# Opening of a fused attention, MoE and gMLP kernel: weight conversions kept in order on VectorE, the first mixing product on ScalarE, the receive weight later

## The chip, the core and the metric

The kernel runs on one core of one Trainium2 chip. The metric is device time in microseconds (us) of one execution. Three runs of the kernel before gave 469.3, 469.85 and 469.86, so 469.85 is the median. Engines are named as the profile names them: PE is TensorE's matmul and PEld its weight load, DVE is VectorE, ACT is ScalarE, POOL is GpSimd, and SP is the queue that issues the DMAs.

## The reference

Three layers are applied one after another, all in float32, for 4 batches of 1088 tokens.

```python
# attention: 4 heads of 32; S1, S2 are (8, 32)
a, b = S1 @ x, S2 @ x                       # for x = q and x = k
phi(x) = outer(a, b).reshape(64)
kv, z = phi(k).T @ v, phi(k).sum(tokens)
x = (phi(q) @ kv) / (phi(q) @ z + 1e-6)     # joined to 128 columns
# token-mixing MLP; x_prev is x shifted by one token
xk = mu_k * x + (1 - mu_k) * x_prev
xr = mu_r * x + (1 - mu_r) * x_prev
x = sigmoid(xr @ w_r) * (relu(xk @ w_k) ** 2 @ w_v)     # w_k 128x1024, w_v 1024x128
# gMLP
u, v = split(relu(x @ w_in))                # 512 columns each
v = layernorm(v) ; v = w_spatial @ v + b    # w_spatial 1088x1088
out = (u * v) @ w_out
```

The weights of the two MLPs reach the chip as 64-bit floats, and the chip turns each into two 32-bit parts.

## The kernel before

Tokens lie along the columns in chunks of 384, 384 and 320 for each batch, twelve chunks in all, numbered i = 0 to 11. A float32 product is made of three matmuls (`mm3`, line 112): each operand is split into a high part H (a copy in the reduced matmul type) and a low part L (`low`, line 118, the difference), and low times high, high times high and high times low are added in PSUM. Both parts must be there before a triple is complete.

Weights pass through `split64` (lines 120 to 139). For a half of w_k or w_v (128x512) VectorE runs five steps: L125 takes the exponent bits, L127 and L128 gather the low mantissa bits, L129 puts the sign in, L130 makes the power of two. ScalarE turns the exponent around after L125 (line 126), scales the low bits after L128 (line 132) and copies the high part after L129 (line 115). GpSimd multiplies the low part after L130 (line 133). Five conversions matter here: the first and the second half of w_k (tiles k0 for H, k1 for L), the first and the second half of w_v (xs1H, xs1L) and the receive weight w_r (128x128, tiles wrH, wrL; its low part is made on VectorE, line 135).

The attention of chunk i has four steps: `q_feat` makes the outer products from a matmul with the small features (L189, L200), `q_turn` transposes them (L241, ScalarE copies them to tile VR), `q_num` multiplies by the key sums and divides (L258, L262 to L264), `q_out` transposes the result back to xT (L276, ScalarE copies it to tile x). `k_feat` and `k_sum` (L200, L220) do the same for keys. The outer products of the second batch's keys are three GpSimd products of 128x768 each.

`prep(i)` mixes the chunk with its shift and splits it. For chunk 0 `q_out` has also made mu_k * x (L280, `x_mu`), and `prep(0)` needs one more VectorE step (L300) to have xk; its H (m11, ScalarE, L115) and L (m13, VectorE, L118) go to the up matmuls. `prep_r` and `receive` do the same with mu_r and w_r, and `gate` takes the sigmoid.

The middle part counts groups g: `up(g)` multiplies chunk g // 8 by 128 columns of w_k (f = g % 8; f = 0 to 3 need the first half of w_k, f = 4 to 7 the second) into one of three PSUM banks, ScalarE takes the relu (L340). For every other group GpSimd squares it (L343) and `sqsplit` splits it (ScalarE L372, VectorE L118); for the others ScalarE squares it alone (L360) and a sum of both parts of w_v is used (`total_wv`, GpSimd, line 689, tile wvT; L386). `down(g)` follows four groups later and multiplies by w_v. Other work is hung on groups with `plan(g, fn)`; R0 and R1 say at which g the sums wvT, the conversions of the second half of w_v and of w_r and the receive work stand.

The code is not the order on the engines: a scheduling layer orders each engine's instructions with estimates of its own when the kernel is built, and each engine then runs its list strictly in that order. `behind(anchors, fn)` tells that layer not to place what fn records ahead of the anchor instructions in the list of the anchor's engine; it adds no wait on the chip.

Of the kernel before, what the change touches and what calls it, by code (L numbers as in the profile page):

```python
# [11 lines left out]
AF = mybir.ActivationFunctionType  # L12
ALU = mybir.AluOpType
# [45 lines left out]
W1G = 69  # L59
W1N = 8  # L60
ORD0 = ((0, 0), (1, 0), (0, 1), (1, 1), (2, 0), (3, 0), (2, 1), (3, 1), (0, 2), (1, 2), (2, 2), (3, 2))
R0 = (1, 5)
R1 = 5
VW = NH * (HD + 1)


# [1 line left out]
def attn_moe_gmlp(ctx: ExitStack, tc: tile.TileContext, qT, kT, va, st, wk, wv, wr, win, wout,  # L68
                  wT, wtail, btail, mu, ident, msk, out):
    nc = tc.nc  # L70
    TE, VE, SE, GE = nc.tensor, nc.vector, nc.scalar, nc.gpsimd
# [6 lines left out]
    def sb(tag, shape, dt=F32):  # L78
        uid[0] += 1
        return pool.tile(shape, dt, tag=tag, bufs=1, name=f"{tag}_{uid[0]}")  # L80
# [7 lines left out]
    def rot(*tags):  # L88
        i = count.get(tags, 0)
        count[tags] = i + 1  # L90
        return tags[i % len(tags)]
# [12 lines left out]
    mus = sb("mus", [128, 3])  # L104
# [12 lines left out]
    def low(eng, L, src, H):  # L117
        return eng.tensor_tensor(out=L, in0=src, in1=H.bitcast(F32), op=ALU.subtract)  # L118

    def split64(raw, n, H, L, total=None):  # L120
        hi, lo = raw[:, :, 1], raw[:, :, 0]
        x = rot(*CVT)
        th, s = sb(f"w{x + 1}", [128, 2, n], I32), sb(f"w{x + 2}", [128, n], I32)
        t, h = th[:, 0], th[:, 1]
        VE.tensor_scalar(out=t, in0=hi, scalar1=0x7FFFFFFF, scalar2=9, op0=ALU.bitwise_and, op1=ALU.logical_shift_right)  # L125
        SE.activation(out=h, in_=t, func=AF.Relu, scale=4096.0, bias=ebias)
        VE.tensor_scalar(out=s, in0=hi, scalar1=0x1FF, scalar2=15, op0=ALU.bitwise_and, op1=ALU.logical_shift_left)  # L127
        VE.scalar_tensor_tensor(out=s, in0=lo, scalar=17, in1=s, op0=ALU.logical_shift_right, op1=ALU.bitwise_or)  # L128
        VE.scalar_tensor_tensor(out=h, in0=hi, scalar=-0x80000000, in1=h, op0=ALU.bitwise_and, op1=ALU.bitwise_or)  # L129
        VE.tensor_scalar(out=t, in0=h, scalar1=-0x800000, scalar2=None, op0=ALU.bitwise_and)  # L130
        if total is None and n in CONVP:
            SE.activation(out=s.bitcast(F32), in_=s, func=AF.Copy, scale=2.0 ** -35)
            GE.tensor_tensor(out=L, in0=s.bitcast(F32), in1=t.bitcast(F32), op=ALU.mult)  # L133
        else:
            VE.scalar_tensor_tensor(out=L, in0=s, scalar=2.0 ** -35, in1=t.bitcast(F32), op0=ALU.mult, op1=ALU.mult)
        if total is None:
            copy(H, h.bitcast(F32))
        else:
            VE.tensor_tensor(out=total, in0=h.bitcast(F32), in1=L, op=ALU.add)
# [107 lines left out]
    nd_pe, x_copy, x_mu_op = [None], [None], [None]  # L247
# [19 lines left out]
    def q_out(i):  # L267
        b, c = divmod(i, 3)
        o, n = CH[c]
        if c == 0:  # L270
            xTs[b] = sb(f"x{b}", [128, S + 1])
            GE.memset(xTs[b][:, 0:1], 0.0)
        xm = qst.pop(i)
        px = bank(5)
        for t in order3(c):
            x_turn[0] = TE.transpose(px[:, cut(c, t)], xm[:, t].rearrange("p h c -> p (h c)"), idn)  # L276
        x_copy[0] = copy(xTs[b][:, 1 + o:1 + o + n], px[:, :n])
        if i == 0:
            a = x_mu[0] = sb(m(1), [128, n])
            x_mu_op[0] = VE.tensor_scalar(out=a, in0=px[:, :n], scalar1=mus[:, 0:1], scalar2=None, op0=ALU.mult)  # L280


    GL = B * NCH * NF - GLB
    anchor, prep_L = [None, None, None], [None, None]
# [329 lines left out]
    def behind(anchors, fn, *a):  # L614
        with ExitStack() as es:
            for x in anchors:
                es.enter_context(tc.issue_after(x.ins))
            fn(*a)
# [11 lines left out]
    nd_last0 = list(nd_last)  # L630
# [9 lines left out]
    behind(nd_pe0, k_sum, 1, 0, range(3))  # L640
    behind(x_turn0, k_sum, 1, 0, range(3, NT))
    k_sum(1, 1)
    behind(x_mu_op, conv64)
    load64(*wseq[4])
    load_q(1)
    behind(prep_L, conv64)
    prep_0 = list(prep_L) + PG * nd_pe0
    todo = {}

    def plan(g, fn, *a):  # L650
        todo.setdefault(g, []).append(lambda: fn(*a))
# [7 lines left out]
    for j in range(1, NI):  # L659
        sp = 1 if j < 3 else 2  # L660
        for n, fn in enumerate((q_feat, q_turn, q_num, q_out)):
            plan(QS[j] + sp * n, gated(fn) if j < 3 and n == 0 else fn, j)
        e = QS[j] + 3 * sp
        plan(max(8 * j - 6, e + 1), prep, j)
        plan(max(8 * j - 4, e + 2), prep_r, j)
        plan(8 * j - 2, receive, j)
        plan(8 * j - 1, gate, j)
    QE = [QS[3 * b + 2] + 1 for b in range(B)]
    for b in range(1, B):
        last = QS[3 * b]  # L670
# [23 lines left out]
    for n in range(2):  # L694
        plan(R0[n], total_wv, n)
        plan(R0[n], conv_first)
    plan(R1, prep_r, 0)
    plan(R1 + 3, receive, 0)
    plan(R1 + 4, gate, 0)
    for n, x in enumerate(wseq[5:]):  # L700
        plan(C0 - 2 + CS * n, load64, *x)
        plan(C0 + CS * n, conv_late)
# [15 lines left out]
    for g in range(NI * NF + LAG):  # L718
        if g < NI * NF:
            up(g)  # L720
        if g >= LAG:
            down(g - LAG)
        if 1 <= g <= NI * NF:
            sqsplit(g - 1)
        at[0] = g
        for fn in todo.pop(g, ()):
            fn()
# [91 lines left out]
```

## Time and profile before

| | us |
|---|---|
| median of three runs | 469.85 |
| the profiled execution, as timed | 468.91 |
| its span in the trace | 467.1 |
| PE busy in the span | 453.8 (97%) |
| DVE, ACT, POOL busy | 235.4, 239.1, 188.7 |
| PE idle between 20 and 45 us, by windows | 4.87 |
| PE idle between 45 and 467 us, by windows | 6.94 |

The span is one execution as the trace shows it, from the first to the last instruction; the timed execution has 1.81 us around it. Matmuls overlap one another and their ends are modelled, so the length of a row of several matmuls is a little more than the step to the next one. A bracket at the end of a row gives the time for which the engine had nothing to run, and what ended that time.

### The profile page before, as it was taken

How to read it: one execution, taken by the hardware profiler on the slowest of the kernel's cores; microseconds unless marked ns; L12 is line 12 of the kernel's file. 1: busy time of each engine (PE TensorE's matmuls, PEld its weight loads, DVE VectorE, ACT ScalarE, POOL GpSimd, SP SyncE). 2: the span in 40 equal slices, each digit the busy share in tenths (PEclk: the TensorE clock that was granted, in tenths of full speed). 3: DMA queues.
4: the chain of work that ended last, by engine and by line, in shares of the span. 5: the costliest groups of instructions: out<-in, count | busy, mean ns of one | idle time of the engine just before them, and what ended most of it. 6: DMA issues, size and time to landing. Idle time of an engine off the chain costs nothing.

```text
span 467.1 us, 7296 instructions
## 1 busy us (share of the span) xinstructions
PE 453.8 (97%) x2751; PEld 432.4 (93%) x2751; DVE 235.4 (50%) x424; ACT 239.1 (51%) x565; POOL 188.7 (40%) x244
## 2 busy tenths in 40 slices
PE   8978999999999999999999999999999999999997
PEld 8967998888998988999999999999999999999996
DVE  5598867687755795448633435521335421212121
ACT  2585868887877877675327423441433441312111
POOL 2566546684564596556217313440213430200000
PEclk9999999999999999999999999999999999999999
DMA  7972100122100000032000000000100000000001
GB/s 232 351 238 93 49 0 19 35 68 76 36 18 1 1 0 2 17 88 74 1 17 18 15 0 1 0 2 0 49 1 1 0 1 17 32 1 0 1 1 48
DMA packets 12227, 18.77 MB, mean 40 GB/s; under 512 B 1760, under 2 KB 10784, under 8 KB 12192
## 3 DMA queue, kind: packets, MB, share of 16 engines
q1 hardware_dynamic: 12192, 18.31, 12.3%
q8 instruction: 21, 0.34, 0.3%
q14 instruction: 14, 0.11, 0.1%
HBM read 16.08 MB, written 2.23 MB: 39 GB/s over the span
## 4 chain that ended last, share of the span: by engine, by line
PE 61%; DVE 0%; ACT 0%; issue 0%; DVEq 0%; ACTq 0%
PE p L112 56%; PE p L511 2%; PE p L512 2%; PE p L386 1%; DVE w L118 0%; PE p L540 0%; ACT m L115 0%; ACT w L372 0%; DVEq L118 0%; ACTq L115 0%
## 5 line engine op out<-in xcount | busy, mean ns | idle before, releaser
L516 DVE TENSOR_TENSOR m<-p,m 128x384 f32<-128x384 f32 (+1 forms) x43 | 22.9, 532 | 96.4 <-PE p L512 92.2
L112 PE MATMUL p<-m,k 128*128 128x384 f32 (+1 forms) x288 | 67.8, 353 | 3.4 <-POOL k L133 1.6
L503 ACT ACTIVATE m<-p 128x384 f32<-128x384 f32 (+1 forms) x44 | 20.6, 469 | 78.4 <-PE p L112 76.4
L343 POOL TENSOR_TENSOR m<-m 128x384 f32<-128x384 f32 (+1 forms) x48 | 42.7, 896 | 41.7 <-ACT m L340 39.9
L112 PEld LDWEIGHTS p<-m,k 128*128 128x128 f32 x288 | 48.3, 188 | 8.7 <-ACT m L340 2.4
L112 PE MATMUL p<-w,m 128*128 128x384 f32 (+1 forms) x288 | 51.6, 327 | 0.0
L112 PE MATMUL p<-w,k 128*128 128x384 f32 (+1 forms) x288 | 51.4, 328 | 0.0
L340 ACT ACTIVATE m<-p 128x384 f32<-128x384 f32 (+1 forms) x96 | 43.2, 468 | 12.8 <-PE p L112 9.9
L112 PE MATMUL p<-w,n1H 128*128 128x384 f32 (+1 forms) x192 | 48.7, 330 | 0.0
L112 PEld LDWEIGHTS p<-w,m 128*128 128x128 f32 x288 | 48.0, 188 | 0.4
L112 PE MATMUL p<-w,n0H 128*128 128x384 f32 (+1 forms) x192 | 48.2, 329 | 0.0
L112 PEld LDWEIGHTS p<-w,k 128*128 128x128 f32 x288 | 47.9, 188 | 0.3 <-ACT k L115 0.2
L118 DVE TENSOR_TENSOR m<-m,m 128x384 fp32r<-128x384 f32 (+1 forms) x47 | 28.8, 614 | 37.8 <-ACT m L115 30.9
L118 DVE TENSOR_TENSOR w<-m,w 128x384 fp32r<-128x384 f32 (+1 forms) x44 | 36.1, 826 | 22.7 <-ACT w L372 11.8
L112 PEld LDWEIGHTS p<-w,n1H 128*128 128x128 f32 x192 | 34.3, 188 | 1.3
L112 PEld LDWEIGHTS p<-w,n0H 128*128 128x128 f32 x192 | 34.2, 188 | 0.6
L386 PE MATMUL p<-w,wvT 128*128 128x384 f32 (+1 forms) x88 | 34.3, 471 | 0.0
L450 ACT ACTIVATE VR<-p 128x512 f32<-128x512 f32 x32 | 18.9, 596 | 28.7 <-PE p L112 27.2
L456 POOL TENSOR_SCALAR rs<-mv 128x1 f32<-128x1 f32 x32 | 7.4, 232 | 60.3 <-DVE mv L455 59.4
L112 PE MATMUL p<-w,n0L 128*128 128x384 f32 (+1 forms) x96 | 31.8, 331 | 0.0
L112 PE MATMUL p<-w,n1L 128*128 128x384 f32 (+1 forms) x96 | 31.5, 328 | 0.0
L458 DVE TENSOR_SCALAR VR<-VR,mv,rs 128x512 f32<-128x512 f32 x32 | 20.0, 625 | 16.8 <-POOL rs L457 16.5
(193 smaller groups left out, 1028.7 us busy)
## 6 DMA issues: line engine op xcount, KB each, us to landing
st<-in_wT_dram SPq DMA_DIRECT2D x16, 192.0 KB, 2.4
w<-in_kT_dram SPq DMA_DIRECT2D x8, 192.0 KB, 5.0
w<-in_qT_dram SPq DMA_DIRECT2D x8, 192.0 KB, 4.6
out_dram<-m SPq DMA_DIRECT2D x8, 192.0 KB, 1.9
st<-in_wT_dram SPq DMA_DIRECT2D x8, 160.0 KB, 2.2
xs0H<-in_va_dram SPq DMA_DIRECT2D x2, 528.0 KB, 5.8
xs0L<-in_va_dram SPq DMA_DIRECT2D x2, 528.0 KB, 6.6
w<-in_wk_dram SPq DMA_DIRECT2D x2, 512.0 KB, 6.7
```

Source lines behind the costliest of these rows:

```text
L112: TE.matmul(out_ap, lhsT=l, rhs=r, start=first and n == 0, stop=last and n == 2)
L118: return eng.tensor_tensor(out=L, in0=src, in1=H.bitcast(F32), op=ALU.subtract)
L340: SE.activation(out=r, in_=hk, func=AF.Relu)
L343: anchor[2] = GE.tensor_tensor(out=sq, in0=r, in1=r, op=ALU.mult)
L386: TE.matmul(vvs[i], lhsT=wvT[:, f // 2], rhs=hls.pop(g), start=f == 0, stop=f == NF - 1)
L450: SE.activation(out=v, in_=pv, func=AF.Relu)
L456: GE.tensor_scalar(out=rs, in0=mv[:, 1:2], scalar1=1e-6, scalar2=None, op0=ALU.add)
L458: VE.tensor_scalar(out=v, in0=v, scalar1=mv[:, 0:1], scalar2=rs, op0=ALU.subtract, op1=ALU.mult)
L503: SE.activation(out=u, in_=pu, func=AF.Relu)
L511: TE.matmul(acc, lhsT=T2, rhs=wtile(NK, c)[1], start=False, stop=False)
L512: TE.matmul(acc, lhsT=T1, rhs=wtile(NK, c)[0], start=False, stop=True)
L516: VE.tensor_tensor(out=u, in0=acc, in1=u, op=ALU.mult)
```

## The change

The second half of w_k is converted behind the last division of chunk 0 (`nd_last0`) where it stood behind L280, and L280 itself goes to ScalarE. The conversion of the first half of w_v is held behind the last VectorE step (L130) of the second half of w_k, and the first split of an up group (`sqsplit(0)`) behind the L130 of the first half of w_v. The second sum wvT, the conversion of w_r and `prep_r(0)` move from group 5 to group 7; `receive(0)` stays at group 8 and `gate(0)` at 9, and for later chunks `prep_r` comes no earlier than group 9, `receive` than 10 and `gate` than 11. In the new file the lines are 1 to 5 higher (L118 is L119, L125 is L128, L280 is L283, L300 is L303, L133 is L136, L343 is L346).

```diff
@@ -59,8 +59,9 @@
 W1G = 69
 W1N = 8
 ORD0 = ((0, 0), (1, 0), (0, 1), (1, 1), (2, 0), (3, 0), (2, 1), (3, 1), (0, 2), (1, 2), (2, 2), (3, 2))
-R0 = (1, 5)
-R1 = 5
+R0 = (1, 7)
+R1 = 7
+RJ = 10
 VW = NH * (HD + 1)
 
 
@@ -116,6 +117,8 @@
 
     def low(eng, L, src, H):
         return eng.tensor_tensor(out=L, in0=src, in1=H.bitcast(F32), op=ALU.subtract)
+
+    conv_t = [None]
 
     def split64(raw, n, H, L, total=None):
         hi, lo = raw[:, :, 1], raw[:, :, 0]
@@ -127,7 +130,7 @@
         VE.tensor_scalar(out=s, in0=hi, scalar1=0x1FF, scalar2=15, op0=ALU.bitwise_and, op1=ALU.logical_shift_left)
         VE.scalar_tensor_tensor(out=s, in0=lo, scalar=17, in1=s, op0=ALU.logical_shift_right, op1=ALU.bitwise_or)
         VE.scalar_tensor_tensor(out=h, in0=hi, scalar=-0x80000000, in1=h, op0=ALU.bitwise_and, op1=ALU.bitwise_or)
-        VE.tensor_scalar(out=t, in0=h, scalar1=-0x800000, scalar2=None, op0=ALU.bitwise_and)
+        conv_t[0] = VE.tensor_scalar(out=t, in0=h, scalar1=-0x800000, scalar2=None, op0=ALU.bitwise_and)
         if total is None and n in CONVP:
             SE.activation(out=s.bitcast(F32), in_=s, func=AF.Copy, scale=2.0 ** -35)
             GE.tensor_tensor(out=L, in0=s.bitcast(F32), in1=t.bitcast(F32), op=ALU.mult)
@@ -277,7 +280,7 @@
         x_copy[0] = copy(xTs[b][:, 1 + o:1 + o + n], px[:, :n])
         if i == 0:
             a = x_mu[0] = sb(m(1), [128, n])
-            x_mu_op[0] = VE.tensor_scalar(out=a, in0=px[:, :n], scalar1=mus[:, 0:1], scalar2=None, op0=ALU.mult)
+            x_mu_op[0] = SE.activation(out=a, in_=px[:, :n], func=AF.Copy, scale=mus[:, 0:1])
 
 
     GL = B * NCH * NF - GLB
@@ -640,10 +643,12 @@
     behind(nd_pe0, k_sum, 1, 0, range(3))
     behind(x_turn0, k_sum, 1, 0, range(3, NT))
     k_sum(1, 1)
-    behind(x_mu_op, conv64)
+    behind(nd_last0, conv64)
+    wk2_t = list(conv_t)
     load64(*wseq[4])
     load_q(1)
-    behind(prep_L, conv64)
+    behind(prep_L + wk2_t, conv64)
+    wv1_t = list(conv_t)
     prep_0 = list(prep_L) + PG * nd_pe0
     todo = {}
 
@@ -662,9 +667,9 @@
             plan(QS[j] + sp * n, gated(fn) if j < 3 and n == 0 else fn, j)
         e = QS[j] + 3 * sp
         plan(max(8 * j - 6, e + 1), prep, j)
-        plan(max(8 * j - 4, e + 2), prep_r, j)
-        plan(8 * j - 2, receive, j)
-        plan(8 * j - 1, gate, j)
+        plan(max(8 * j - 4, e + 2, RJ - 1), prep_r, j)
+        plan(max(8 * j - 2, RJ), receive, j)
+        plan(max(8 * j - 1, RJ + 1), gate, j)
     QE = [QS[3 * b + 2] + 1 for b in range(B)]
     for b in range(1, B):
         last = QS[3 * b]
@@ -695,8 +700,8 @@
         plan(R0[n], total_wv, n)
         plan(R0[n], conv_first)
     plan(R1, prep_r, 0)
-    plan(R1 + 3, receive, 0)
-    plan(R1 + 4, gate, 0)
+    plan(R1 + 1, receive, 0)
+    plan(R1 + 2, gate, 0)
     for n, x in enumerate(wseq[5:]):
         plan(C0 - 2 + CS * n, load64, *x)
         plan(C0 + CS * n, conv_late)
@@ -721,7 +726,7 @@
         if g >= LAG:
             down(g - LAG)
         if 1 <= g <= NI * NF:
-            sqsplit(g - 1)
+            behind(wv1_t if g == 1 else (), sqsplit, g - 1)
         at[0] = g
         for fn in todo.pop(g, ()):
             fn()
```

VectorE behind the end of chunk 0's division (L264); w_81 and w_82 belong to the second half of w_k, w_85 and w_86 to the first half of w_v, mx_246 is xk and m_66 its low part. Before:

```order
L280 TENSOR_SCALAR m_62_243<-p_61_238,mus_64 128x384
L125 TENSOR_SCALAR w_81_311<-w_36_144 128x512
L127 TENSOR_SCALAR w_82_312<-w_36_144 128x512
L300 SCALAR_TENSOR_TENSOR mx_246<-x_60_236,mus_64,m_62_243 128x384
L128 SCALAR_TENSOR_TENSOR w_82_312<-w_36_144,w_82_312 128x512
L129 SCALAR_TENSOR_TENSOR w_81_311<-w_36_144,w_81_311 128x512
L118 TENSOR_TENSOR m_66_250<-mx_246,m_65_249 128x384
L125 TENSOR_SCALAR w_85_328<-w_38_150 128x512
L127 TENSOR_SCALAR w_86_329<-w_38_150 128x512
L225 TENSOR_TENSOR kb_80_309<-p_79_290,mk_63 128x132
L200 TENSOR_TENSOR n1L_347<-p_91_348,bs_92_352 128x768
L130 TENSOR_SCALAR w_81_311<-w_81_311 128x512
```

Now:

```order
L128 TENSOR_SCALAR w_81_311<-w_36_144 128x512
L130 TENSOR_SCALAR w_82_312<-w_36_144 128x512
L131 SCALAR_TENSOR_TENSOR w_82_312<-w_36_144,w_82_312 128x512
L132 SCALAR_TENSOR_TENSOR w_81_311<-w_36_144,w_81_311 128x512
L303 SCALAR_TENSOR_TENSOR mx_246<-x_60_236,mus_64,m_62_243 128x384
L133 TENSOR_SCALAR w_81_311<-w_81_311 128x512
L119 TENSOR_TENSOR m_66_250<-mx_246,m_65_249 128x384
L128 TENSOR_SCALAR w_85_328<-w_38_150 128x512
```

The L280 row is gone, the first four steps of the second half of w_k stand ahead of the mixing step, and the fifth (L130 on w_81, now L133) ahead of the low part m_66 where it was five rows behind it.

ScalarE in the same place; p_61 is the transposed result of chunk 0, x_60 its copy, m_62 the mixing product, m_65 the high part of xk, k_10 the high part of w_k. Before:

```order
L115 ACTIVATE x_60_236<-p_61_238 128x384
L126 ACTIVATE w_81_311<-w_81_311,ebias_66 128x512
L115 ACTIVATE m_65_249<-mx_246 128x384
L115 ACTIVATE bs_92_352<-p_91_348 128x96
L132 ACTIVATE w_82_312<-w_82_312 128x512
L115 ACTIVATE k_10_75<-w_81_311 128x512
L126 ACTIVATE w_85_328<-w_85_328,ebias_66 128x512
L340 ACTIVATE m_88_343<-p_87_339 128x384
```

Now:

```order
L129 ACTIVATE w_81_311<-w_81_311,ebias_66 128x512
L116 ACTIVATE x_60_236<-p_61_238 128x384
L283 ACTIVATE m_62_243<-p_61_238,mus_64 128x384
L135 ACTIVATE w_82_312<-w_82_312 128x512
L116 ACTIVATE k_10_75<-w_81_311 128x512
L116 ACTIVATE m_65_249<-mx_246 128x384
L116 ACTIVATE bs_92_352<-p_91_348 128x96
L129 ACTIVATE w_85_328<-w_85_328,ebias_66 128x512
L343 ACTIVATE m_88_343<-p_87_339 128x384
```

The exponent step of the second half of w_k stands ahead of the copy of x, the mixing product behind that copy, and the high part of xk (m_65) behind the two other conversion steps.

GpSimd from the last key product on; k_11 is the low part of the second half of w_k, m_89 and m_102 are squares, xs1L is the low part of w_v's first half. Before:

```order
L200 TENSOR_TENSOR w_73_269<-m_75_274 128x768
L301 TENSOR_TENSOR m_63_245<-x_60_236 128x384
L343 TENSOR_TENSOR m_89_345<-m_88_343 128x384
L133 TENSOR_TENSOR k_11_76<-w_82_312,w_81_311 128x512
L343 TENSOR_TENSOR m_102_392<-m_101_390 128x384
L133 TENSOR_TENSOR xs1L_78<-w_86_329,w_85_328 128x512
```

Now:

```order
L203 TENSOR_TENSOR w_73_269<-m_75_274 128x768
L304 TENSOR_TENSOR m_63_245<-x_60_236 128x384
L136 TENSOR_TENSOR k_11_76<-w_82_312,w_81_311 128x512
L346 TENSOR_TENSOR m_89_345<-m_88_343 128x384
L346 TENSOR_TENSOR m_102_392<-m_101_390 128x384
L136 TENSOR_TENSOR xs1L_78<-w_86_329,w_85_328 128x512
```

The low part of the second half of w_k moves ahead of the first square.

VectorE around the conversion of w_r (w_125, w_126 before; w_129, w_130 now); w_98 is the second half of w_v, w_121 and w_137 (now w_128) are low parts of squares, mx_436 is xk of chunk 1. Before:

```order
L130 TENSOR_SCALAR w_98_375<-w_98_375 128x512
L263 RECIPROCAL de_105_403<-de_105_403 128x12
L264 TENSOR_TENSOR VR_61<-p_104_396,de_105_403 128x384
L118 TENSOR_TENSOR w_121_450<-m_112_427,w_121_450 128x384
L125 TENSOR_SCALAR w_125_460<-w_83_322 128x128
L127 TENSOR_SCALAR w_126_461<-w_83_322 128x128
L128 SCALAR_TENSOR_TENSOR w_126_461<-w_83_322,w_126_461 128x128
L129 SCALAR_TENSOR_TENSOR w_125_460<-w_83_322,w_125_460 128x128
L130 TENSOR_SCALAR w_125_460<-w_125_460 128x128
L118 TENSOR_TENSOR w_137_500<-m_132_482,w_137_500 128x384
L135 SCALAR_TENSOR_TENSOR wrL_81<-w_126_461,w_125_460 128x128
L298 SCALAR_TENSOR_TENSOR mx_436<-m_115_435,mus_64,x_60_236 128x384
```

Now:

```order
L132 SCALAR_TENSOR_TENSOR w_98_375<-w_78_288,w_98_375 128x512
L267 TENSOR_TENSOR VR_61<-p_104_396,de_105_403 128x384
L133 TENSOR_SCALAR w_98_375<-w_98_375 128x512
L119 TENSOR_TENSOR w_121_450<-m_112_427,w_121_450 128x384
L119 TENSOR_TENSOR w_128_473<-m_124_459,w_128_473 128x384
L128 TENSOR_SCALAR w_129_477<-w_83_322 128x128
L130 TENSOR_SCALAR w_130_478<-w_83_322 128x128
L131 SCALAR_TENSOR_TENSOR w_130_478<-w_83_322,w_130_478 128x128
L132 SCALAR_TENSOR_TENSOR w_129_477<-w_83_322,w_129_477 128x128
L133 TENSOR_SCALAR w_129_477<-w_129_477 128x128
L138 SCALAR_TENSOR_TENSOR wrL_81<-w_130_478,w_129_477 128x128
L301 SCALAR_TENSOR_TENSOR mx_436<-m_115_435,mus_64,x_60_236 128x384
```

The low part of the second square is now ahead of the five steps of w_r, and the last step of the second half of w_v (L130, now L133) is behind the division (L264, now L267) where it stood two rows ahead of it.

## Rows read from the trace of the kernel before

**Rows 1.** Windows: stretch, length, busy PE, PEld, DVE, ACT, POOL; clock, DMA share, GB/s.
```profile
20.00:45.00 25.00, 20.13 (x134) 17.44 (x134) 23.45 (x38) 16.83 (x40) 15.95 (x13) 1.00 0.59 199
45.00:467.00 422.00, 415.06 (x2491) 396.46 (x2489) 202.59 (x363) 215.34 (x510) 164.07 (x206) 1.00 0.06 19
```

**Rows 2.** Timeline of TensorE: start, length, line, out<-in, count, [idle before <-releaser].
```profile
22.75 1.91 PE L112 MATMUL p<-m,k 128*128 128x384 f32 x9
...
25.34 0.80 PE L112 MATMUL p<-m,k 128*128 128x384 f32 x3 [0.68 <-ACT m L340]
...
29.06 1.83 PE L112 MATMUL p<-m,k 128*128 128x384 f32 x9 [1.60 <-POOL k L133]
...
32.84 0.45 PE L112 MATMUL p<-w,xs1L 128*128 128x384 f32 x1 [0.60 <-POOL xs1L L133]
...
34.13 0.87 PE L241 MATMUL p<-idn,n1L 128*128 128x128 f32 x6 [0.49 <-DVE n1L L200]
...
38.10 0.42 PE L112 MATMUL p<-w,xs1L 128*128 128x384 f32 x1
...
38.72 0.83 PE L189 MATMUL p<-Sbd,w 128*128 128x128 f32 x6
...
42.05 0.44 PE L112 MATMUL p<-w,xs1H 128*128 128x384 f32 x1 [1.50 <-DVE w L118]
...
45.56 1.29 PE L112 MATMUL p<-m,k 128*128 128x384 f32 x6
```

**Rows 3.** Timeline of VectorE, same columns.
```profile
18.13 0.56 DVE L264 TENSOR_TENSOR VR<-p,de 128x384 f32<-128x384 f32 x1
...
20.13 0.62 DVE L280 TENSOR_SCALAR m<-p,mus 128x384 f32<-128x384 f32 x1 [1.44 <-ACT x L115]
...
23.27 0.54 DVE L118 TENSOR_TENSOR m<-mx,m 128x384 fp32r<-128x384 f32 x1
...
23.74 0.41 DVE L125 TENSOR_SCALAR w<-w 128x512 int32<-128x512 int32 x1
...
27.81 1.61 DVE L118 TENSOR_TENSOR w<-m,w 128x384 fp32r<-128x384 f32 x1 [0.72 <-POOL m L343]
...
29.34 1.05 DVE L125 TENSOR_SCALAR w<-w 128x512 int32<-128x512 int32 x1
...
31.58 1.62 DVE L118 TENSOR_TENSOR w<-m,w 128x384 fp32r<-128x384 f32 x1
...
35.17 0.43 DVE L130 TENSOR_SCALAR w<-w 128x512 int32<-128x512 int32 x1
...
38.94 1.50 DVE L128 SCALAR_TENSOR_TENSOR w<-w,w 128x128 int32<-128x128 int32 x1
```

**Rows 4.** Timeline of GpSimd, same columns.
```profile
15.38 4.44 POOL L200 TENSOR_TENSOR w<-m 128x768 f32<-128x768 f32 x3
...
25.43 2.35 POOL L343 TENSOR_TENSOR m<-m 128x384 f32<-128x384 f32 x1 [4.43 <-ACT m L340]
...
27.74 1.26 POOL L133 TENSOR_TENSOR k<-w,w 128x512 fp32r<-128x512 f32 x1
...
28.96 1.14 POOL L343 TENSOR_TENSOR m<-m 128x384 f32<-128x384 f32 x1
...
33.76 0.83 POOL L343 TENSOR_TENSOR m<-m 128x384 f32<-128x384 f32 x1
...
38.78 1.51 POOL L200 TENSOR_TENSOR n1L<-sab 128x768 f32<-128x768 f32 x1
```

**Rows 5.** Timeline of ScalarE, same columns.
```profile
19.60 0.49 ACT L115 ACTIVATE x<-p 128x384 f32<-128x384 f32 x1 [2.96 <-PE p L276]
...
21.32 0.72 ACT L126 ACTIVATE w<-w,ebias 128x512 int32<-128x512 int32 x1 [1.22 <-DVE w L125]
...
22.17 0.52 ACT L115 ACTIVATE m<-mx 128x384 fp32r<-128x384 f32 x1
...
24.18 0.72 ACT L126 ACTIVATE w<-w,ebias 128x512 int32<-128x512 int32 x1 [0.17 <-DVE w L125]
```

## The prediction

> **What bounds the kernel now.** I read the windows first. TensorE is the engine that sets the end: from 20 to 45 us it is busy 20.13 of 25.00 us, and in the 422 us after that it is idle for only 6.94 [rows 1]. The 4.87 us of idle time in the opening are what this change can win. In the same 25 us VectorE is busy for 23.45, so it has almost nothing left to give [rows 1].
>
> TensorE's timeline says who ends each pause [rows 2]. There are five: 0.68 for the relu of the first up group (at 25.34), 1.60 for the low part of w_k's second half (29.06), 0.60 for the low part of w_v's first half (32.84), 0.49 for an outer product (34.13), 1.50 for the low part of a square (42.05). They sum to 4.87.
>
> The timelines of VectorE and GpSimd are to be read side by side. L118 takes 0.54 alone (at 23.27) and 1.61 at 27.81; it then ends at 29.42, 0.42 behind the end of GpSimd's L133 (27.74 + 1.26 = 29.00) [rows 3, 4]. L125 takes 0.41 alone (23.74) and 1.05 at 29.34, ending at 30.39, 0.29 behind GpSimd's L343 (28.96 + 1.14 = 30.10) [rows 3, 4]. L343 at 25.43 in turn takes 2.35 while VectorE works without a gap [rows 4]. So a GpSimd product and a VectorE step on SBUF tiles run one after the other. The Trainium skill's GPSIMD Engine Reference (Specifications) says that the SBUF interfaces are shared with VectorE, in contention with its instructions in a 2-port mode or with two SBUF inputs; the trace agrees with the 1.61 against 0.54. Without this contention step 1 below would cost nothing and the sum would be 0.65 better.
>
> **The change, step by step.** The times are those of the profiled execution.
>
> Step 1, the start of up(0). L125 of w_k's second half can now start when L264 ends, 18.13 + 0.56 = 18.69, and not at 20.7, behind L280 [rows 3]. But GpSimd's three L200 run from 15.38 to 19.82 [rows 4], so L125 ends about 0.29 later, at 20.1. ScalarE's list now has L126 (0.72) ahead of the copy of x, which starts at 20.8 and not at 19.60 [rows 5]. The copy takes 0.49, so x is there at 21.3. The product on ScalarE isn't in the trace: it reads the same tile as the copy (0.49), and a 512-column step with a per-partition operand takes 0.72 [rows 5]; I take 0.6, nearer the copy, against 0.62 on VectorE. L300, a step of the same 384 columns as L280 (0.62), ends at 22.5. The high part m11 (0.52) now stands behind two conversion steps on ScalarE of at most 0.72 each, so it ends between 23.2 and 23.9; I take 23.4. TensorE starts up(0) at 22.75 today [rows 2], just when m11 ends (22.17 + 0.52 = 22.69) [rows 5]. Cost 0.65, between 0 (L125 not held) and 1.1.
>
> Step 2, w_k's low part. L130 now follows L300: about 22.95. L133 (1.26) ends at 24.2, where TensorE wants it after 28. The 1.60 goes. L118 for m13 is asked for at 23.4, stands behind that L133 and ends 0.42 behind it, at 24.6. TensorE wants it after six of the nine matmuls (1.91), at 24.7: no wait.
>
> Step 3, the first relu. It still stands behind L126 of w_v's first half, which waits for its L125. L125 ends at 24.6 + 0.41 = 25.05, L126 at 25.8, against 24.18 + 0.72 = 24.90 today [rows 5]. So up(3) moves from 25.34 to 26.2, and as TensorE is free at 23.4 + 1.91 = 25.3, the wait is 0.9 instead of 0.68: cost 0.2. up(4) follows 29.06 - 1.60 - 25.34 = 2.1 later, at 28.3: gain so far 0.75.
>
> Step 4, w_v's first half. From L125's end VectorE has L127, L200, a small L225, L128, L129 and L130, which last 3.4 without GpSimd and 5.1 with two squares of 0.83 (33.76) between them [rows 4]; then L133, 1.26. It ends between 29.7 and 31.4. TensorE asks at 28.3 + (32.84 - 0.60 - 29.06 = 3.2) = 31.5. The 0.60 goes; gain 1.35.
>
> Step 5, the next low part and the outer product. Today VectorE needs 5.4 us from L118 at 27.81 to the end of L118 at 31.58 + 1.62 = 33.20 [rows 3]. L130 (0.43) and L128 (0.7) are no longer between the two, and 1.2 was the wait for w_k's L133: 3.1 stay. From the middle of step 4's end of L130, 29.3, that is 32.4; TensorE wants it at 33.1. Cost 0, up to 1.0 if GpSimd gets in between every time. L128 and L200 follow until 34.0, wanted at 34.65, so the 0.49 goes too. Without a further wait down(4) would come at 31.5 + (38.10 - 32.84 - 0.49 = 4.8) = 36.3.
>
> Step 6, w_v's second half. Its L130 ran at 35.17 [rows 3]. It now stands behind L200, L262, L263, L129 and L264, 2.1 us in all, and ends at 36.1; L133 makes it 37.4. So down(4) waits 1.1 for it, a new wait, between 0.3 and 2.0. down(4) comes at 37.4, where it was 38.10: gain 0.7.
>
> Step 7, the receive weight. Its five steps no longer stand ahead of L118 for w6, on which the 1.50 rests; the longest of them takes 1.50 for 128 columns, behind a GpSimd L200 of 1.51 [rows 3, 4]. After L133 come L118 (37.85), the sum wvT on GpSimd (half of L133's columns: 0.63 to 1.26, I take 0.7; 38.6) and L118 (39.15). The sum makes L386 wait 0.6, the L118 nothing. down(6) needed 42.05 - 38.10 = 3.95 with the wait of 1.50 and a group of six L189 (0.83 long, a step of 0.7), which now comes behind: 1.75 + 0.6 makes 39.75. The way to up(8) is 45.56 - 42.05 = 3.5 plus 0.7: 43.95. Chunk 1's m12 needs the receive steps done: 39.15, two GpSimd products (1.5 and 0.9), six steps of 0.2, L298 and the copy (1.1) give 43.9. Gain at up(8): 45.56 - 43.95 = 1.6.
>
> Sum: -0.65 - 0.2 + 1.6 + 0.6 + 0.5 - 1.1 - 0.6 + 1.5 = 1.65, say 1.6. The loads are no term: w_r's is merely issued earlier, and no row waits for one here. From up(8) on the matmuls are the same and TensorE stays the bound, so the gain is kept, except that the lists differ to the end: a reshuffle of the 6.94 us idle there may give or take 1. The profiled execution took 468.91 (467.1 and 1.81 around it), so 467.3; the median was 0.94 above it, so I forecast 469.85 - 1.6 = 468.3. With every bound at its good end the sum is 1.65 + 0.65 + 0.2 + 0.8 + 0.6 = 3.9; at the bad end 1.65 - 0.45 - 0.2 - 1.0 - 0.5 = -0.5.
>
> **Rivals.** First, VectorE paces the opening and a better order on TensorE is hidden: its 23.45 of 25 us [rows 1] lose only L280, 0.62. Then up(8) is 0.6 earlier at most: 469.25. For it speak that steps 1, 3 and 6 are all VectorE's list against GpSimd; against it, that the 1.50 hangs on where L118 stands, not on VectorE's total.
>
> Second, slower. The receive steps now stand directly ahead of chunk 1's L298, at a place where GpSimd has two 128x768 products and the mixing difference to run. If four of the six wait 1.5 each [rows 3], L298 starts at 39.15 + 6.4 = 45.5, and m12 is there at 46.7: TensorE waits at up(8), 1.15 later than today, with nothing else to run: 471.0. It decides if L298 starts after 44.4. The row of 1.50 speaks for it; against it, GpSimd's second product waits for a ScalarE copy that now stands behind w_r's own high part, so GpSimd is likely to pause.
>
> Third, all waits go: L125 slips in at 18.69 and steps 3, 6 and 7 cost nothing; 3.9 better, 465.95. Rows 3 and 4 speak against it.
>
> **Numbers.** Forecast (gain 0.9 to 2.7) 0.45; all waits gone 0.11; hidden 0.25; slower 0.19. Faster or slower means by over 0.2%, 0.94 us, about what a measurement of this kernel can tell from no change. The forecast and the third rival give faster 0.55 (a sliver lies within the bound), the hidden case same 0.26, the second slower 0.19. The range reaches from most of the third rival, 466.2, to most of the second, 470.9; the forecast's own is 467.2 to 468.9.
>
> **What would show it.** The copy of x starts at 20.8, behind L126; if it starts before 20, step 1 is wrong. No pause of TensorE ends on w_k's L133 or on the L118 that stood behind the receive steps. A new pause of about 1 us ends on w_v's second L133, at 37. up(8), the first matmuls on m12, starts near 44. The prediction is wrong if up(8) starts after 45, or if it starts near 44 and the pauses behind 45 us grow by over 1 us.

## The result and the profile after

The changed kernel took 472.48 us (median of 7 runs, 471.02 to 474.47); the kernel before, run beside it, 469.49 (7 runs, 469.19 to 469.86). The ratio is 1.0067, 95% interval 1.0053 to 1.0081: slower by 3.0 us. The forecast was 468.3, in a range of 466.2 to 470.9. The profiled execution of the changed kernel took 474.06 with a span of 472.3.

More line numbers of the changed kernel: L115 is now L116, L189 L192, L200 L203, L264 L267, L298 L301, L340 L343, L386 L389; in the single parts below they lie between.

First the windows of the changed kernel, in the columns of [rows 1]:

```profile
20.00:45.00 25.00, 21.67 (x144) 18.36 (x142) 23.95 (x37) 17.78 (x42) 15.45 (x14) 1.00 0.61 202
45.00:467.00 422.00, 414.04 (x2475) 395.87 (x2474) 198.33 (x361) 214.60 (x508) 163.40 (x206) 1.00 0.06 18
```

The opening is better: TensorE is busy 1.54 us more in these 25 us. The rest is worse: 1.02 less in the same 422 us, and the span goes on to 472.3, where it ended at 467.1. TensorE's timeline of the opening answers to [rows 2]:

```profile
23.86 1.32 PE L113 MATMUL p<-m,k 128*128 128x384 f32 x6 [0.61 <-ACT m L116]
25.49 0.80 PE L113 MATMUL p<-m,k 128*128 128x384 f32 x3 [0.30 <-DVE m L119]
26.96 0.79 PE L113 MATMUL p<-m,k 128*128 128x384 f32 x3 [0.67 <-ACT m L343]
...
31.77 0.44 PE L113 MATMUL p<-w,xs1L 128*128 128x384 f32 x1
...
38.78 0.44 PE L113 MATMUL p<-w,xs1L 128*128 128x384 f32 x1 [1.31 <-POOL xs1L L136]
...
39.79 0.91 PE L389 MATMUL p<-w,wvT 128*128 128x384 f32 x2 [0.22 <-POOL wvT L694]
...
44.98 1.30 PE L113 MATMUL p<-m,k 128*128 128x384 f32 x6
```

The waits on w_k's low part (1.60), on w_v's first low part (0.60), on the outer product (0.49) and on the L118 behind the receive steps (1.50) are gone; new ones are 1.31 on w_v's second low part, 0.61 on m11, 0.30 on m13 and 0.22 on the sum wvT. Up(8) starts at 44.98, before at 45.56. This profile is late from the start: its rows from 9.7 to 23 us come 0.33 to 0.41 later than the same rows before, after a wait of 0.85 for a load at 8.34, which other profiles have in other sizes, 0 to 1.1. I take 0.36 for it, so the opening is worth 0.58 + 0.36 = 0.94.

The largest loss is one place at 118 us. TensorE's timeline there:

```profile
115.06 0.49 PE L279 MATMUL p<-idn,VR 128*128 128x128 f32 x3
118.21 1.75 PE L113 MATMUL p<-m,k 128*128 128x320 f32 x5 [2.66 <-ACT m L343]
```

The spatial weight comes in pieces through two staging buffers, st0 and st1, in turn: a load fills the buffer, ScalarE copies the high part into a weight tile (w0, w2 and so on), and GpSimd or VectorE makes the low part. ScalarE's timeline, two of these staged copies and the relu behind them:

```profile
112.25 0.52 ACT L116 ACTIVATE w<-st 128x384 fp32r<-128x384 f32 x1 [1.53 <-DMA st<-in_wT_dram]
...
117.31 0.52 ACT L116 ACTIVATE w<-st 128x384 fp32r<-128x384 f32 x1 [3.24 <-DMA st<-in_wT_dram]
117.74 0.42 ACT L343 ACTIVATE m<-p 128x320 f32<-128x320 f32 x1
```

The chain of waits (start, duration, what) says why the copy waited:

```profile
112.25 0.53 ACT w L116
...
112.85 1.03 POOL w L119
...
113.90 3.39 DMA st<-in_wT_dram
...
117.31 0.03 ACT w L116
...
117.74 0.43 ACT m L343
...
118.21 1.75 PE p L113 x5
```

The copies at 112.25 and 117.31 fill tiles w0 and w2, and both read the staging buffer st1. The load for tile w2 can go out only when GpSimd has made w0's low part from it (113.88), and takes 3.39. The copy into w2 stands ahead of a relu in ScalarE's list, ScalarE takes its list in order, and TensorE wants that relu. The windows by one microsecond (length, busy PE, PEld, DVE, ACT, POOL; clock; DMA share; GB/s) show a second price, the clock:

```profile
117.00:118.00 1.00, 0.00 (x0) 0.00 (x0) 0.14 (x1) 0.69 (x2) 0.00 (x0) 1.00 0.00 0
118.00:119.00 1.00, 0.79 (x3) 0.75 (x4) 1.00 (x2) 1.00 (x4) 0.03 (x1) 0.66 0.00 0
119.00:120.00 1.00, 1.00 (x6) 1.00 (x5) 1.00 (x2) 1.00 (x4) 0.69 (x1) 0.50 0.43 101
120.00:121.00 1.00, 1.00 (x6) 1.00 (x6) 0.73 (x2) 0.99 (x4) 0.26 (x1) 0.50 0.26 95
121.00:122.00 1.00, 1.00 (x7) 0.92 (x6) 0.00 (x0) 0.67 (x3) 0.46 (x1) 0.64 0.00 0
122.00:123.00 1.00, 1.00 (x8) 0.84 (x6) 0.05 (x1) 1.00 (x4) 0.85 (x1) 1.00 0.00 0
```

Behind the pause the granted clock is at its lower level, 1.2 GHz, for about three microseconds. By these windows that costs an estimated 1.6 us of work (the part of the clock that is missing, times the busy time), on top of the 2.66. It does not come in every execution: three of the seven have a mean granted clock of 1.0 and took 471.02, 471.69 and 472.30, all above the slowest run before (469.86); the other four, the profiled one among them, have 0.993 to 0.996 and took 472.48 to 474.47. So the kernel is slower without the lower clock too, and this profile shows more than the median loss.

In the kernel before these copies were further apart. Its ScalarE timeline there, with another copy that waits for its load:

```profile
110.79 0.52 ACT L115 ACTIVATE w<-st 128x384 fp32r<-128x384 f32 x1 [2.04 <-DMA st<-in_wT_dram]
...
115.72 0.52 ACT L115 ACTIVATE w<-st 128x384 fp32r<-128x384 f32 x1 [0.46 <-DMA st<-in_wT_dram]
...
120.18 0.53 ACT L115 ACTIVATE w<-st 128x384 fp32r<-128x384 f32 x1 [0.15 <-DMA st<-in_wT_dram]
```

In ScalarE's list the copies into w0 and w2 stand ten rows apart before (195 and 205, at 115.72 and 120.18) and five now (191 and 196). Nothing in the diff touches them: the scheduler places them as the list ahead of them falls.

The table sets the profiles side by side: the start of TensorE's n-th matmul less that of the kernel before, in us (a timeline row of several matmuls is divided evenly). A matmul of 66 columns counts here like one of 384, and the lists place them differently, so a middle row can be off by a microsecond or more. The profiles also start apart: at matmul 40 the columns read +0.36, +0.17, -0.40, -0.37, +0.20 and +0.44. The columns' kernels come in the next section.

| matmul (us before) | changed | e1 no load | e4 one copy | e2 hold | p4 no receive | e6 the same, hold |
|---|---|---|---|---|---|---|
| 280 (47) | -0.92 | -0.89 | -1.31 | -0.89 | -0.24 | +0.11 |
| 720 (117) | -1.94 | -2.03 | -2.50 | -3.19 | -1.89 | -2.71 |
| 760 (123) | +1.33 | -2.24 | -3.08 | -4.12 | -2.44 | -3.45 |
| 1000 (162) | +3.09 | -0.81 | -1.63 | -3.30 | +0.24 | -2.10 |
| 1150 (191) | +2.83 | -1.05 | -1.83 | -1.28 | -1.15 | +1.44 |
| 1300 (218) | +4.82 | +0.79 | -1.32 | -0.96 | -0.69 | +3.58 |
| 2650 (442) | +4.82 | +0.96 | -0.89 | -1.11 | -0.69 | +3.58 |

The changed kernel leads by 1.9 us at 117 us, loses 3.3 by this count at the one pause (2.66 + 1.6 = 4.3 by its own rows) and 2.0 more between 191 and 218 us; behind 218 its column stays. That it moves by 1.8 between matmuls 760 and 1000 is the order of short and long matmuls and no loss: from 124 to 162 us TensorE is busy for 38.00 of 38.00 us in both kernels.

### The profile page after: what moved, and what is told of

Same layout as the page of the kernel before. It is cut to its first block, busy times and chain, and to the rows that moved or that the text cites. A ratio compares the mean times of both kernels' runs of the same rounds, so it can differ in the third digit from the quotient of the medians.

```text
span 472.3 us, 7300 instructions
## 1 busy us (share of the span) xinstructions
PE 455.5 (96%) x2751; PEld 433.0 (92%) x2751; DVE 233.1 (49%) x423; ACT 239.8 (51%) x566; POOL 187.3 (40%) x244
## 4 chain that ended last, share of the span: by engine, by line
PE 79%; DVE 7%; DMA 4%; POOL 4%; ACT 3%; issue 2%; SPq 0%; POOLq 0%; ACTq 0%; DVEq 0%
PE p L113 64%; PE p L389 4%; DMA st<-in_wT_dram 3%; PE p L261 2%; PE p L192 2%; DVE w L119 2%; PE p L514 2%; PE p L223 2%; PE p L515 2%; DMA w<-in_qT_dram 1%; PE p L244 1%; POOL w L119 1%; ACT w L116 1%; DVE w L128 1%; ACT m L343 1%
## 5 line engine op out<-in xcount | busy, mean ns | idle before, releaser
L113 PE MATMUL p<-m,k 128*128 128x384 f32 (+1 forms) x288 | 65.8, 349 | 4.5 <-ACT m L343 3.6
L346 POOL TENSOR_TENSOR m<-m 128x384 f32<-128x384 f32 (+1 forms) x48 | 43.2, 905 | 41.5 <-ACT m L343 38.8
L343 ACT ACTIVATE m<-p 128x384 f32<-128x384 f32 (+1 forms) x96 | 43.2, 472 | 10.0 <-PE p L113 9.2
L119 DVE TENSOR_TENSOR m<-m,m 128x384 fp32r<-128x384 f32 (+1 forms) x47 | 29.3, 624 | 33.1 <-ACT m L116 30.9
L119 DVE TENSOR_TENSOR w<-m,w 128x384 fp32r<-128x384 f32 (+1 forms) x44 | 34.5, 794 | 20.7 <-POOL m L346 12.0
L389 PE MATMUL p<-w,wvT 128*128 128x384 f32 (+1 forms) x88 | 34.5, 474 | 0.3 <-POOL wvT L694 0.2
L459 POOL TENSOR_SCALAR rs<-mv 128x1 f32<-128x1 f32 x32 | 8.6, 268 | 58.9 <-DVE mv L458 58.0
```

Source lines behind the costliest of these rows:

```text
L113: TE.matmul(out_ap, lhsT=l, rhs=r, start=first and n == 0, stop=last and n == 2)
L343: SE.activation(out=r, in_=hk, func=AF.Relu)
L346: anchor[2] = GE.tensor_tensor(out=sq, in0=r, in1=r, op=ALU.mult)
L389: TE.matmul(vvs[i], lhsT=wvT[:, f // 2], rhs=hls.pop(g), start=f == 0, stop=f == NF - 1)
```

## The experiments

Medians are of the kernel named; its ratio is to the kernel before, run beside it (469.2, 469.38 or 469.35 by batch; 469.49 beside the changed kernel). The diffs are cut to the lines that matter.

**The three parts apart.** The order of the conversions alone (p1), the product on ScalarE alone (p2), the receive weight's place alone (p3).

```diff
p1  -    behind(x_mu_op, conv64)
    +    behind(nd_last0, conv64)          # wk2_t, wv1_t and sqsplit as in the change
p2  -            x_mu_op[0] = VE.tensor_scalar(out=a, in0=px[:, :n], ...)
    +            x_mu_op[0] = SE.activation(out=a, in_=px[:, :n], func=AF.Copy, scale=mus[:, 0:1])
p3  -R0 = (1, 5)
    -R1 = 5
    +R0 = (1, 7)
    +R1 = 7
    +RJ = 10                               # and the three plan lines that use it
```

> The order of the weight conversions alone (product back on VectorE, receive work back at group 5). Late-order theory: the opening is near the changed kernel's, up(8) about 45.0, and the time is not set there but by what ScalarE's list does between 110 and 130 us: the staged copy for tile w2 stands 11 rows behind the one for w0 (5 rows in the changed kernel), so no pause over 1.5 us near 118 and no lowered clock; 469 to 470.5. Opening theory (the steps I had counted as gains are losses): 471 or more, already lost before 60 us.

> The mixing product on ScalarE alone. Late-order theory: the copy for w2 stands 10 rows behind that for w0, no pause over 1.5 us near 118, 469 to 470.5. Opening theory: the product moved to ScalarE delays the first up groups, 470.5 to 472.

> The receive weight, its sum and the receive steps later, alone. Late-order theory: the 1.50 us pause at 42 goes, the copy for w2 stands 10 rows behind that for w0, no pause over 1.5 us near 118, 468 to 470. Receive theory (gates that come later hold back the products behind down): pauses ending on the gate or on xr and 471 or more.

p1: 468.17, ratio 0.9972 (0.9962 to 0.9983), faster. p2: 468.9, 0.9994 (0.9985 to 1.0002), no difference that can be told. p3: 470.36, 1.0026 (1.0015 to 1.0036), slower. The sum of the three differences is -1.03 - 0.3 + 1.16 = -0.2; together they gave +3.0. So the loss is not the sum of the parts. None of the three has a pause over 1.5 us near 118, as expected; the times were not: p1 is below both of its ranges, p2 just below its first, and p3 between its two.

p3 alone shows what the second rival of the prediction had in mind, but not its price. Its TensorE timeline, then VectorE's:

```profile
45.35 1.31 PE L113 MATMUL p<-m,k 128*128 128x384 f32 x6 [1.04 <-ACT m L116]
```

```profile
39.44 1.53 DVE L126 TENSOR_SCALAR w<-w 128x128 int32<-128x128 int32 x1
40.89 0.86 DVE L128 TENSOR_SCALAR w<-w 128x128 int32<-128x128 int32 x1
41.78 1.64 DVE L129 SCALAR_TENSOR_TENSOR w<-w,w 128x128 int32<-128x128 int32 x1
...
44.13 0.61 DVE L299 SCALAR_TENSOR_TENSOR mx<-m,mus,x 128x384 f32<-128x384 f32 x1
```

Three of the six receive steps are stretched beside GpSimd's products (1.82 at 39.06, 0.82 at 40.84, 1.50 at 41.77), L299 (L301 of the changed kernel) starts at 44.13, just ahead of the 44.4 from which that rival decides, and up(8) waits 1.04. It still starts 0.21 earlier than before (45.35 against 45.56), so the 1.16 that p3 loses come later; its longest waits there are 1.30 at 74.98 (0.91 before) and 1.20 at 110.57, and no run takes them apart. In the changed kernel L301 starts at 42.83 and up(8) waits for nothing.

**The load taken away (e1).** The changed kernel leaves out the load for w2 and makes the tile from the columns staged for w0. ScalarE's copy into w2 moves up with it, directly behind that into w0; the other staged copies keep their rows to within six.

```diff
+        if (k, c) == (3, 1):
+            pending_raw.append((k, c, kept[0]))
+            rot("st0", "st1")
+            return
```

> The changed kernel with the one load left out on which ScalarE waits 3.24 us at 114 to 117: tile w2 is made from the staged columns of tile w0, so that part of the spatial weight is not the reference's; the lists are otherwise nearly the same. Late-order theory: the pause of 2.66 us and the lowered clock behind it go, the lead of 1.9 us at 115 is still there at 125, and the time is 3 to 4 us under the changed kernel's: 468.5 to 469.5. Symptom theory (ScalarE or the next product would have been late in any case): another wait takes its place, 471.5 or more.

470.49, ratio 1.0036 (1.0022 to 1.005): 2.0 less than the changed kernel. The pause at 116.29 is 0.35, and the lead is 2.24 at matmul 760, where the changed kernel is 1.33 behind. By the medians the wait for that load is worth 2.0; the two profiled executions lie 3.94 apart (474.06 and 470.12), and only the changed kernel's has the lower clock there. The time is between the two expectations (468.5 to 469.5, and 471.5 or more): the pause went without another in its place, but the loss at 191 to 218 us stays (1.84 in the table).

**Pairs of parts.** The change without its receive part (p4), and without the product on ScalarE (p5); their diffs are those of the change less p3's or p2's lines.

> The changed kernel without its receive part (receive weight and receive steps back at group 5). Its lists are those of the kernel with the product alone from about 60 us on; they differ only in the opening, where the conversions keep their order. So the difference of the two is the order alone, under one tail. Late-order theory: the opening is up to 1 us better, no pause over 1.5 us near 118, 467.8 to 469. Opening theory: the order costs, 469.5 or more.

> The changed kernel without the product on ScalarE. Late-order theory: the copy for w2 stands 11 rows behind that for w0 (5 in the changed kernel), so no pause over 1.5 us near 118; 468 to 470.5. Receive theory: with the receive part in it stays at 471 or more.

p4: 468.25, 0.9972 (0.9962 to 0.9983). p5: 469.15, 0.9991 (0.998 to 1.0003). Both are in their first range, and neither has a pause of 2 us. Of the combinations that were run only the three parts together put the copy into w2 five rows behind that into w0 (10 or 11 in the others); the product with the receive part alone was not run. None of the parts can be blamed by itself.

**The staged copies held back (e2, and e3 as its control).** The copies of eight groups are listed behind the anchors (the last square on each engine) of the group that plans them; the opening is untouched. e2 holds them in the changed kernel, e3 in the kernel before.

```diff
+    def wstep_held():
+        behind([x for x in anchor if x is not None], wstep)
+
     for n in range(W1N):
-        plan(W1G + n, wstep)
+        plan(W1G + n, wstep_held)
```

> The changed kernel with the copies of the second column third of the spatial weight held behind the last square of groups 69 to 76 on each engine, where they are planned, and not let forward. Late-order theory: no wait of ScalarE for a staged load ahead of a relu between 105 and 130, the pause of 2.66 is gone, 469 to 470.5, near the run without the one load. Symptom theory: 471.5 or more.

> The kernel before with the same hold, the control for the run above. Late-order theory: it loses a little from where the copies now stand or stays within 0.5 of 469.2; the changed kernel with the hold is within 1.5 of it and no longer 3 us slower. Symptom theory: the changed kernel with the hold stays 2.5 us or more slower than this one.

e2: 467.93, 0.9971 (0.9962 to 0.998), 4.6 less than the changed kernel, faster than the kernel before and below the 469 to 470.5 that were expected. e3: 469.43, 1.0001 (0.9991 to 1.0011): worth nothing there. Under the same hold the change gains 469.43 - 467.93 = 1.5 in this pair; as the hold lays out the lists anew (e6 below), that is not the worth of the opening alone.

**One copy held (e4).** Only the copy into w2 is held: row 196 goes to row 289 of ScalarE's list, the other staged copies keep theirs to within three rows.

```diff
-        copy(H, src)
+        if (k, c) == (3, 1):
+            late(copy, H, src)
+        else:
+            copy(H, src)
```

> The changed kernel, in which one instruction alone is held back: ScalarE's copy of the staged spatial weight into w2 keeps its place behind the last product group, so in ScalarE's list it moves from row 196 to row 289 and all other staged copies keep their places to within three rows (w3's from 207 to 210). Theory (that copy, standing ahead of a relu while its load runs, costs the pause of 2.66 us and the lowered clock behind it): the pause at 118 us falls below 0.5, the lead at matmul 760 is near -2 us against before as without that load (-2.24 there), and the time is about 470.5, 2 below the changed kernel; the loss of some 2 us between 190 and 215 us stays. Rival (the copies stand too close as a group, and the wait only passes to the next of them, w3's): a pause of over 1 us shows behind w3's copy, and the time stays at 471.5 or above.

468.64 (467.78 to 469.69, 11 runs), 0.9986 (0.9977 to 0.9994): 3.8 less than the changed kernel, about twice what was expected. Its windows where the changed kernel had 0.66, 0.50 and 0.50:

```profile
118.00:119.00 1.00, 1.00 (x12) 1.00 (x11) 0.49 (x1) 1.00 (x4) 0.58 (x2) 1.00 0.00 0
119.00:120.00 1.00, 1.00 (x11) 1.00 (x10) 0.89 (x1) 1.00 (x5) 1.00 (x2) 1.00 0.00 0
120.00:121.00 1.00, 1.00 (x10) 1.00 (x10) 0.09 (x1) 1.00 (x3) 1.00 (x1) 1.00 0.00 0
```

TensorE does not stop there, and the loss between 191 and 218 us is gone too. It is a pause in the changed kernel's TensorE timeline:

```profile
214.72 0.41 PE L113 MATMUL p<-m,xs1H 128*128 128x320 f32 x1 [1.29 <-DVE m L119]
```

VectorE's list of the same kernel has a staged tile's low part ahead of that square's:

```profile
212.39 0.80 DVE L119 TENSOR_TENSOR w<-st,w 128x320 fp32r<-128x320 f32 x1 [4.18 <-ACT w L116]
213.11 1.55 DVE L119 TENSOR_TENSOR m<-m,m 128x320 fp32r<-128x320 f32 x1
```

With the copy gone from row 196 the list from 191 us on was laid out anew, and no square waits there. So moving one instruction is worth 3.8 us by the medians: 2.0 is its wait (e1), and the rest, some 1.8, goes with the loss from 191 to 218 us, of which the pause at 214 is the largest piece. That pause is not tied to that copy: e1 has the same pause (1.13 at 210.69) without the load, and e6 below (1.14 at 213.48) with the copy held. What puts VectorE's low part ahead of the square stays open; no run moved it.

**More held (e5), and the hold on other kernels (e6, e7).** e5 has e2's hold on the next eight steps too (the line shown, beside e2's); e6 is p4 and e7 p1, each with e2's hold.

```diff
e5  -        plan(GL + GW + n, wstep)
    +        plan(GL + GW + n, wstep_held)
```

> The changed kernel with the hold of the earlier run on the staged copies of groups 69 to 76, and the same hold on those of the eight groups behind GL + GW (tiles w4 to w7 and the first of the last chunk's). In the run with the first hold alone the lead over before was 3.60 us at matmul 960 and 1.28 at 1150; 2.3 us went between 155 and 190 us. Theory (the second set of staged copies shares those places with the first and takes the gain back): with it held as well the lead at 1150 stays above 2, and the time is 466.8 to 467.4. Rival (the first set, which the hold itself moved to 157 to 175 us, takes it back alone): nothing changes up to 1150 and the time stays near 467.9. Against both: the second set is wanted soon after, so held further it could make TensorE wait behind 215 us: above 468.5.

> The changed kernel without its receive part (the order of the conversions and the product on ScalarE stay, the receive weight stands where it stood before), with the hold on the staged copies of groups 69 to 76. Without the hold it took 468.25, 1.1 below the kernel before; its lead was 3.74 us at matmul 600 and 0.7 at the end, so some 3 us went between 97 and 160 us. Theory (the staged copies in the tail take back what the opening gains, in this kernel too): the hold keeps more of it, 467.2 to 467.8. Rival (the hold was worth 4.5 us in the changed kernel only because that one had a bad place, and is worth nothing here as it was worth nothing in the kernel before, 469.43 against 469.38): 468.2 to 468.4.

> The order of the conversions alone (product on VectorE, receive weight where it stood before) with the hold on the staged copies of groups 69 to 76. Without the hold it took 468.17. Theory (each opening keeps its gain once the copies stand clear of the relus): 467.3 to 467.9. Rival (the hold is worth nothing where no copy stood badly): 468.1 to 468.4. Between this run and the one with the product on ScalarE, the theory of the opening says that the product is worth at most 0.6 (one step of 0.62 off VectorE), so their times lie within 0.6 of each other.

e5: 468.52, 0.9988 (0.9978 to 0.9997), not the 466.8 to 467.4 of the theory. Its lead falls from 3.96 at matmul 1000 to 1.74 at 1150, much as in e2 (3.30 to 1.28). That fits the rival, in which the first set takes the gain back, but no run isolates it, and the time is 0.6 above the rival's 467.9. e7: 468.86, 0.9993 (0.9984 to 1.0001); both expectations were too low. e6: 471.95 (470.67 to 472.96, 6 runs), 1.0052 (1.0036 to 1.0068): 3.7 slower than p4 without the hold. Theory and rival were both wrong on it, and e6 and e7 lie 3.1 apart where at most 0.6 was expected. TensorE's timeline of e6:

```profile
180.09 0.66 PE L514 MATMUL p<-w,T 128*128 128x384 f32 x1 [2.06 <-POOL T L118]
```

GpSimd's:

```profile
176.90 1.14 POOL L345 TENSOR_TENSOR m<-m 128x384 f32<-128x384 f32 x1
178.00 1.30 POOL L118 TENSOR_TENSOR w<-st,w 128x384 fp32r<-128x384 f32 x1
179.38 1.48 POOL L118 TENSOR_TENSOR T<-VR,T 64x128 fp32r<-64x128 f32 x3
```

And the clock (length, busy PE, clock, DMA share, GB/s):

```profile
179.00:180.00 1.00, 0.00 (x0) 1.00 0.21 75
180.00:181.00 1.00, 0.91 (x3) 0.57 0.53 152
181.00:182.00 1.00, 1.00 (x5) 0.50 0.13 45
182.00:183.00 1.00, 1.00 (x4) 0.50 0.08 16
183.00:184.00 1.00, 1.00 (x4) 0.72 0.00 0
```

It looks like the changed kernel's loss on another engine. A held low part of a staged tile (178.00) stands on GpSimd ahead of the low part of T, a tile that TensorE's next matmul (L514) reads; TensorE pauses for 2.06 and then runs three to four microseconds at the lower clock. The low part took 1.30, so it can explain at most 1.3 of the 2.06; the profile's own chain names a relu of ScalarE that ends at 179.35 as what released T, and no run moved either. Another 2.1 go between 191 and 218 us, with the pause of 1.14 on a square. That the hold helped e2 and hurt e6 shows that holding by itself is no cure.

## Why the prediction was wrong

It forecast a gain of 1.6 and the kernel lost 3.0.

**The step that failed** is the one sentence behind the sum: "From up(8) on the matmuls are the same and TensorE stays the bound, so the gain is kept, except that the lists differ to the end: a reshuffle of the 6.94 us idle there may give or take 1." The new lists took 3.8: so much less is the time with one copy moved out of the way (e4). The bound of 1 had no row behind it. It was sized by the idle time of the kernel before, as if a new order could only spend that again. But a wait that was hidden before can come onto TensorE's path at its own size: 2.66 here, with a clock at half speed behind it in this execution, of which the profile before shows nothing in its span. The sentence ahead of it failed with it: "The loads are no term: w_r's is merely issued earlier, and no row waits for one here." That holds for the rows of the opening. At 110.79, in the kernel before, ScalarE already waits 2.04 for a staged load, and it was such a load that came onto the path. None of the rivals had a place behind 45 us, so the slower case was named (471.0) by a mechanism that did not happen: L301 starts at 42.83, ahead of the 44.4 from which that one decides.

**The opening, step by step**, with the 0.36 of the late start taken off where steps are compared. Step 1 was right: L128 of w_k's second half ends at 20.50, 0.29 behind GpSimd's L203, and the copy of x starts at 21.16, 20.80 without the late start, as forecast. VectorE's and ScalarE's rows:

```profile
19.01 1.49 DVE L128 TENSOR_SCALAR w<-w 128x512 int32<-128x512 int32 x1
```

```profile
20.53 0.72 ACT L129 ACTIVATE w<-w,ebias 128x512 int32<-128x512 int32 x1 [3.49 <-DVE w L128]
21.16 0.47 ACT L116 ACTIVATE x<-p 128x384 f32<-128x384 f32 x1
21.53 0.57 ACT L283 ACTIVATE m<-p,mus 128x384 f32<-128x384 f32 x1
```

The product took 0.57 for 0.6, and up(0) came 0.75 later for 0.65. Steps 2 and 3: w_k's wait is gone, but L119 for m13 took 1.59 beside GpSimd's L136 and made a wait of 0.30 that step 2 had excluded, and up(3) came 1.26 later where steps 1 and 3 made 0.85. Step 4 was right: down(0) is 1.43 earlier, for 1.35. Step 6 was mis-sized by 1.0: down(4) is 0.32 later, where it was to be 0.7 earlier. VectorE's and GpSimd's last steps for w_v's second half:

```profile
36.72 0.42 DVE L133 TENSOR_SCALAR w<-w 128x512 int32<-128x512 int32 x1
```

```profile
37.28 1.45 POOL L136 TENSOR_TENSOR xs1L<-w,w 128x512 fp32r<-128x512 f32 x1 [2.00 <-DVE w L133]
```

Without the late start L133 ends at 36.78 for the 36.1 forecast, and L136 at 38.37 for 37.4: VectorE came later, and the product took 1.45 for 1.26. Step 7 gave 1.26 for 0.9 (from down(4) to up(8) TensorE needs 6.20 where it needed 7.46): the 1.50 went, and the wait for the sum was 0.22 and not 0.6. In all 0.94 for 1.6. One reading of the prediction is off, with nothing resting on it: VectorE does not work without a gap beside the L343 of 2.35, but idles for its last 0.7 [rows 3].

**Put together**: e4, with that copy out of the way, is 0.7 faster than the kernel before, and the copy back in its place costs 3.8; that makes the 3.0 to within the batches' differences. The first rival (the opening is hidden, 469.25) is not what happened either: up(8) came 0.94 earlier, more than the 0.6 that it allows, and p1, p4, e2 and e4 are faster than the kernel before by 0.7 to 1.5 (p2 and p5 by 0.3 and 0.2, which can't be told from nothing).

What was said would prove it wrong was half right: up(8) at 44.98 is just inside its bound of 45, and by the windows TensorE's idle time between 45 and 467 us grew by 1.02, just over the 1 that it names.

## What to carry to other kernels

A change to a stage that a scheduler orders is priced in two parts, the stage and the lists behind it. For the second, look in the new order at each instruction that waits for a load or a rotating buffer (here the staged copies): if it moved closer to the one before it on the same buffer, or ahead of an instruction that TensorE wants, the price to expect is a wait for that load as the trace shows it (3.24 for ScalarE here, 2.66 for TensorE) and not the idle time of before, and some microseconds at the lower clock may follow. Before a change is dropped as slower, move that one instruction: here it turned 472.48 into 468.64, and the order of the conversions alone (468.17) or the change with the copies of eight groups held (467.93) beat both kernels. Then look again, since every such edit lays the lists out anew: the same hold made p4 3.7 slower.

## What the runs showed of the hardware

The clock fell after short pauses, but not after all of them. In the changed kernel 2.66 us of idle TensorE was followed by 0.66, 0.50, 0.50 and 0.64. e7 and p1 have the same two pauses in the opening: 1.20 and 1.06 for m11, at 24.50 and 24.48, and 1.60 in both for a square's low part, at 41.47 and 41.51. Here are a microsecond behind each in the windows, of e7 and then of p1:

```profile
25.00:26.00 1.00, 1.00 (x5) 1.00 (x5) 1.00 (x3) 0.19 (x1) 0.03 (x1) 0.50 1.07 396
42.00:43.00 1.00, 1.00 (x7) 1.00 (x6) 0.73 (x2) 0.37 (x1) 0.00 (x0) 0.50 0.26 70
```

```profile
25.00:26.00 1.00, 1.00 (x8) 1.00 (x6) 1.00 (x3) 0.21 (x1) 0.00 (x1) 1.00 1.05 381
42.00:43.00 1.00, 1.00 (x11) 1.00 (x10) 0.78 (x2) 0.70 (x4) 0.00 (x0) 1.00 0.42 94
```

After the same 1.60 the clock is at 0.50 in one and at 1.00 in the other; e7's profiled execution is its slowest, 470.42 against a median of 468.86.

What it can cost shows in runs of one kernel: e6 took 470.67 to 471.26 in its three runs with a mean clock of 0.999 or 1.0, and 472.65 to 472.96 in the three with 0.996. It is not always a price: p1's two runs with 0.995 took 467.62 and 467.74, below its median, and p5's two fastest (467.48 and 468.03) have 0.996. Why the clock falls in some executions of the same program and not in others, these runs don't show.
